# A linear-attention and gated-GLU training step on one core: features on partitions, folded attention values, one fused last layer, weight gradients at the end

## The chip, the core and the metric

The kernel runs on one core of a Trainium2 chip. The metric is the device time in microseconds (us). Runs of one kernel are compared through runs of the kernel before on the same chip in the same rounds. The ratios use fast runs alone.

## The reference, cut to what matters

Four layers are applied in turn to `x` of 2048 tokens by 512 features: linear attention (A), GLU (B), A, B. Both A layers share their weights, and so do both B layers. The kernel returns the output and the gradients of the input and of all five weights.

```python
def _A_ref(x, wqkv, wo):                   # 32 heads of 16
    q, k, v = ...                          # x @ wqkv
    phi = lambda t: where(t > 0, t + 1, exp(t)) + 1e-6
    kv = einsum("bhsd,bhse->bhde", phi(k), v)     # a sum over ALL tokens
    z = phi(k).sum over tokens                    # the same
    num, den = phi(q) @ kv, phi(q) @ z + 1e-6
    return (num / den) @ wo
def _B_ref(x, w_gate, w_up, w_down):       # 512 -> 1376 -> 512
    return (sigmoid(x @ w_gate) * (x @ w_up)) @ w_down
x = x + _A_ref(_layernorm(x), ...)         # layer 0
x = x + _B_ref(_layernorm(x), ...)         # layer 1
x = x + _A_ref(_layernorm(x), ...)         # layer 2
x = x + _B_ref(_layernorm(x), ...)         # layer 3
_out, _vjp = jax.vjp(f, ...); _grads = _vjp(grad_out)
```

What matters for the order of work: the attention sums run over all tokens. Nothing of layer 0's values can be finished before its keys are done for the last token, and the backward of an attention has two such sums as well. A program therefore falls into sweeps over the tokens with a seam between each two.

## The kernel before

It keeps tokens on partitions and takes 128 tokens at a time. Each matmul that contracts over features needs a turned operand, so activations and gradients are turned by TensorE with an identity, and ScalarE or VectorE copies them out of PSUM.

```python
def b_fwd(k, l, ln, ...):                       # one GLU layer, forward
    ...
        tps = ps_tp2.tile([P, 4, P], BF16, name="hhT_ps")
        for i, fc in enumerate(fcs):            # TensorE turns hh, 128 columns each
            nc.tensor.transpose(tps[0:r, i, :], hh_t[:, fc * P:fc * P + r], k.ident[:])
        nc.scalar.copy(hhT[:, fcs[0]:fcs[0] + nfull, :], tps[:, 0:nfull, :])
    ...
            nc.scalar.activation(ssd_t[:, 0, c0:c0 + w], g_ps[:, 0:w], ACT.Sigmoid)
            nc.scalar.activation(oms[:, 0:w], g_ps[:, 0:w], ACT.Sigmoid, scale=-1.0)
            nc.vector.tensor_tensor(hh_t[:, c0:c0 + w], u_ps[:, 0:w], ssd_t[:, 0, c0:c0 + w], ALU.mult)
            nc.gpsimd.tensor_tensor(ssd_t[:, 1, c0:c0 + w], hh_t[:, c0:c0 + w], oms[:, 0:w], ALU.mult)
    # [cut] ssd and hh are stored, and loaded again in the backward of the same layer

def p2_cols_group(k, R, lhs_all, set_t, W, dwp2d, out2d, c0, final):   # weight gradients of ONE layer
    if final:                                   # the second layer reloads the first one's partial sums
        R.eng().dma_start(out=av, in_=dwp2d[:, c0:c0 + W].rearrange("(c p) f -> p c f", p=P))
    # [cut] 16 matmuls per PSUM group, one per 128 tokens
        if not final:
            nc.scalar.copy(av[:, half * 2:half * 2 + 2, :], psv)
        else:
            nc.vector.tensor_tensor(ov[...], psv, av[...], ALU.add)
```

Of the kernel before, what the change touches and what calls it, by code (L numbers as in the profile page):

```python
# [11 lines left out]
ALU = mybir.AluOpType  # L12
AX = mybir.AxisListType
# [7 lines left out]
DH = 16  # L21
P = 128
NST = S // P
NDC = D // P
NFC = (F + P - 1) // P
FLAST = F - (NFC - 1) * P
FSL = [(0, 512), (512, 512), (1024, F - 1024)]
EPS_LN = 1e-5
EPS = 1e-6
NB = 4  # L30


def fchunks_of_slice(fs):
    c0, w = FSL[fs]
    return list(range(c0 // P, (c0 + w + P - 1) // P))


def fc_rows(fc):
    return FLAST if fc == NFC - 1 else P


def rows(st):
    return slice(st * P, (st + 1) * P)


class K:
    pass


@with_exitstack  # L50
def kernel(
# [18 lines left out]
    phases = "all"  # L70
    nc = tc.nc
    assert tuple(A_x.shape) == (1, S, D) and tuple(grad_out.shape) == (1, S, D)
    assert tuple(A_wqkv.shape) == (D, 3 * D) and tuple(A_wo.shape) == (D, D)
    assert tuple(B_w_gate.shape) == (D, F) and tuple(B_w_up.shape) == (D, F) and tuple(B_w_down.shape) == (F, D)
    k = K()
    k.nc, k.tc = nc, tc
    k.phases = phases

    x_in = A_x.rearrange("b s d -> (b s) d")
    g_in = grad_out.rearrange("b s d -> (b s) d")  # L80
    out0 = out_0.rearrange("b s d -> (b s) d")
    out1 = out_1.rearrange("b s d -> (b s) d")
# [3 lines left out]
    resid = ctx.enter_context(tc.tile_pool(name="resid", bufs=1))  # L86
    keep = ctx.enter_context(tc.tile_pool(name="keep", bufs=1))
    dram = ctx.enter_context(tc.tile_pool(name="dram", bufs=1, space=DRAM))
    k.keep = keep

    build_consts(k, consts)

    k.xs = [resid.tile([P, D], F32, name=f"x{st}") for st in range(NST)]

    def load_stream(io, src2d, b):
        stg_t = io.tile([P, NB, D], BF16, name="io_in")
        if b == 0:
            nc.sync.dma_start(out=stg_t[:, 0, :], in_=src2d[0:P, :])
            nc.sync.dma_start(out=stg_t[:, 1:NB, :],
                              in_=src2d[P:NB * P, :].rearrange("(n p) d -> p n d", p=P))  # L100
        else:
            nc.sync.dma_start(out=stg_t[:], in_=dram_batch(src2d, b))
        for j in range(NB):
            st = b * NB + j
            if j % 2 == 0:
                nc.vector.tensor_copy(k.xs[st][:], stg_t[:, j, :])
            else:
                nc.scalar.copy(k.xs[st][:], stg_t[:, j, :])
        return stg_t
    k.load_stream = load_stream  # L110

    def store_stream(io, dst2d, b):
        stg_t = io.tile([P, NB, D], BF16, name="io_out")
        for j in range(NB):
            st = b * NB + j
            nc.gpsimd.tensor_scalar(stg_t[:, j, :], k.xs[st][:], 1.0, 0.0, ALU.mult, ALU.add)
        nc.sync.dma_start(out=dram_batch(dst2d, b), in_=stg_t[:])
    k.store_stream = store_stream


    k.sv = {}
    for l in range(4):
        d = {}
        d["h"] = dram.tile([S, D], BF16, name=f"sv_h{l}")
        d["gbf"] = dram.tile([S, D], BF16, name=f"sv_gbf{l}")
        if l % 2 == 0:
            for nm in ("pq", "pk", "v", "o"):
                d[nm] = dram.tile([S, D], BF16, name=f"sv_{nm}{l}")
            d["dqkv"] = dram.tile([S, 3 * D], BF16, name=f"sv_dqkv{l}")
        else:  # L130
            d["ssd"] = dram.tile([S, 2, F], BF16, name=f"sv_ssd{l}")
            d["hdd"] = dram.tile([S, 3, F], BF16, name=f"sv_hdd{l}")
        k.sv[l] = d
    k.wT = dict(
        wqkvT=dram.tile([3 * D, D], BF16, name="wqkvT_d"),
        woT=dram.tile([D, D], BF16, name="woT_d"),
        wgT=dram.tile([F, D], BF16, name="wgT_d"),
        wuT=dram.tile([F, D], BF16, name="wuT_d"),
        wdT=dram.tile([D, F], BF16, name="wdT_d"),
    )  # L140
    k.dwp = dict(
        wqkv=dram.tile([D, 3 * D], BF16, name="dwp_wqkv"),
        wo=dram.tile([D, D], BF16, name="dwp_wo"),
        wg=dram.tile([D, F], BF16, name="dwp_wg"),
        wu=dram.tile([D, F], BF16, name="dwp_wu"),
        wd=dram.tile([F, D], BF16, name="dwp_wd"),
    )
    k.rstd = [keep.tile([P, NST], F32, name=f"rstd_all{l}") for l in range(4)]
    k.kv = {}

    k.A_wo = A_wo
    with tc.tile_pool(name="wfwd", bufs=1) as wfwd:
        k.wqkv = wfwd.tile([P, NDC, 3 * D], BF16, name="wqkv")
        with tc.tile_pool(name="io0", bufs=2) as io:
            load_stream(io, x_in, 0)
            nc.sync.dma_start(out=k.wqkv[:], in_=A_wqkv.rearrange("(c p) j -> p c j", p=P))
            for b in range(1, NST // NB):
                load_stream(io, x_in, b)
        k.wo = wfwd.tile([P, NDC, D], BF16, name="wo")
        nc.sync.dma_start(out=k.wo[:], in_=A_wo.rearrange("(c p) j -> p c j", p=P))  # L160
        k.wg = wfwd.tile([P, NDC, F], BF16, name="wg")
        nc.sync.dma_start(out=k.wg[:], in_=B_w_gate.rearrange("(c p) j -> p c j", p=P))
        k.wu = wfwd.tile([P, NDC, F], BF16, name="wu")
        nc.sync.dma_start(out=k.wu[:], in_=B_w_up.rearrange("(c p) j -> p c j", p=P))
        k.wd = wfwd.tile([P, NFC, D], BF16, name="wd")
        nc.sync.dma_start(out=k.wd[:, 0:NFC - 1, :],
                          in_=B_w_down[0:(NFC - 1) * P, :].rearrange("(c p) j -> p c j", p=P))
        nc.sync.dma_start(out=k.wd[0:FLAST, NFC - 1, :], in_=B_w_down[(NFC - 1) * P:F, :])

        with ExitStack() as lctx:  # L170
            k.lnres = dict(
                stg=lctx.enter_context(tc.tile_pool(name="ln_stg", bufs=2)),
                hT=lctx.enter_context(tc.tile_pool(name="ln_hT", bufs=4)),
                small=lctx.enter_context(tc.tile_pool(name="ln_small", bufs=6)),
                ps=lctx.enter_context(tc.tile_pool(name="ln_ps", bufs=1, space=PSUM)),
            )
            lns = [FwdLN(k, l) for l in range(4)]
            if phases != "fwd":
                wtg = wT_groups(k)
                half = 26  # L180
                with tc.tile_pool(name="wt_stage", bufs=2) as wt_stage:
                    a_fwd(k, 0, lns[0], nxt=lns[1],
                          extra=lambda ps_pool: [g(wt_stage, ps_pool) for g in wtg[:half]])
                b_fwd(k, 1, lns[1], nxt=lns[2])
                with tc.tile_pool(name="wt_stage2", bufs=2) as wt_stage:
                    a_fwd(k, 2, lns[2], nxt=lns[3],
                          extra=lambda ps_pool: [g(wt_stage, ps_pool) for g in wtg[half:]])
            else:
                a_fwd(k, 0, lns[0], nxt=lns[1])
                b_fwd(k, 1, lns[1], nxt=lns[2])  # L190
                a_fwd(k, 2, lns[2], nxt=lns[3])
            ostg = lctx.enter_context(tc.tile_pool(name="out0_stg", bufs=2))
            ocur = {}

            def out_cb(st):
                if st % NB == 0:
                    ocur["t"] = ostg.tile([P, NB, D], BF16, name="out0_t")
                nc.scalar.copy(ocur["t"][:, st % NB, :], k.xs[st][:])
                if st % NB == NB - 1:
                    nc.sync.dma_start(out=dram_batch(out0, st // NB), in_=ocur["t"][:])  # L200
            b_fwd(k, 3, lns[3], out_cb=out_cb)

    if phases == "fwd":
        return
    k.g_in = g_in
    k.g_from_input = 3
    k.sv[3]["gbf"] = g_in

    with ExitStack() as bctx:
        wb = bctx.enter_context(tc.tile_pool(name="wbwd", bufs=1))  # L210
        k.wb = wb

        def load_b_weights():
            k.wdT = wb.tile([P, NDC, F], BF16, name="wdT", tag="w_c")
            nc.sync.dma_start(out=k.wdT[:], in_=k.wT["wdT"].rearrange("(c p) f -> p c f", p=P))
            k.wuT = wb.tile([P, NFC, D], BF16, name="wuT", tag="w_a")
            k.wgT = wb.tile([P, NFC, D], BF16, name="wgT", tag="w_b")
            for t_sb, t_d in ((k.wuT, k.wT["wuT"]), (k.wgT, k.wT["wgT"])):
                nc.sync.dma_start(out=t_sb[:, 0:NFC - 1, :],
                                  in_=t_d[0:(NFC - 1) * P, :].rearrange("(c p) j -> p c j", p=P))  # L220
# [125 lines left out]
def wT_groups(k):  # L346
# [55 lines left out]
    return groups  # L402


NPRE = 2


class FwdLN:
# [701 lines left out]
```

## Time and profile before

| | before |
|---|---|
| time | 1395.17 us, 3 runs, 1393.22 to 1395.18 |
| TensorE matmuls | 9956, 3488 of them of 128 columns, 2840 of these turns with the identity |
| mean granted TensorE clock | 0.988 |

These are lines of the page of the kernel before. The first gives the span, the second each engine's busy time, share and number of instructions (PEld is the weight load, which overlaps PE). The two rows cut the span into 40 slices: busy tenths of TensorE, and the granted clock in tenths. The last row is what the DMA engines moved.

```profile
span 1393.1 us, 25045 instructions
PE 1297.9 (93%) x9956; PEld 790.1 (57%) x9956; DVE 679.9 (49%) x1468; ACT 647.3 (46%) x1168; POOL 250.5 (18%) x413
PE   4989899998899898998999999999999999988988
PEclk9999999999999999999999999999999999999999
DMA packets 268853, 269.77 MB, mean 194 GB/s; under 512 B 24576, under 2 KB 245184, under 8 KB 268736
```

TensorE is the limit. Its busy time overstates the work, since matmuls are pipelined and overlap. So I count *slots*: the distance from one start to the next in undisturbed rows of the timeline, 216 ns for 512 columns, 109 ns for 256 and 57 ns for 128. The 9956 matmuls are then worth about 1233 us. (The Trainium skill, "TensorE: Matmul & The Clock Gate", Part 1, gives N / 2.4 GHz + 2.5 ns, which is 215.7 ns for 512; the trace agrees.) What a stage takes beyond its slots I call its *excess*.

The one large wait of the kernel before lies in its last weight-gradient stage. In the chain of waits (start, length, what) it follows reloads of partial sums, and TensorE's timeline shows the gaps (in brackets: how long it stood idle, and what ended that). The chain runs through these reloads for some 34 us.

```profile
1223.27 9.33 DMA dw_stg<-dwp_wd
...
1235.63 11.10 DMA dw_stg<-dwp_wg
...
1249.65 9.64 DMA dw_stg<-dwp_wd
```

```profile
1233.47 11.94 PE L833 MATMUL p_ps<-p_set,p_a_15354 128*128 128x256 bf16 x96 [4.53 <-DVE dw_stg L798]
...
1260.16 2.08 PE L833 MATMUL p_ps<-p_set,p_a_15354 128*128 128x256 bf16 x9 [5.49 <-DVE dw_stg L798]
```

### The profile page before, as it was taken

Reading aid. Unit: us, or ns where it says so; the run is one execution under the profiler, and the core shown is the slowest. Engines: PE = TensorE matmul, PEld = TensorE weight load, DVE = VectorE, ACT = ScalarE, POOL = GpSimd, SP = SyncE. Lnnn points to the kernel's source line nnn. Section 1 sums busy time; section 2 is a strip of 40 time slices with the busy share of each in tenths; the row PEclk is TensorE's granted clock in tenths of the full one; section 3 lists DMA queues with packets and bytes.
Section 4 is the critical chain, followed back from the end, with each engine's and each line's share of the span. In section 5 each row is a group of like instructions: output and inputs, shape, how many; then the busy total and the mean of one; then the engine's idle time right before and its main releaser. Section 6 shows DMA issues by size and latency. Waiting matters only on the chain. (4 is left out here: it accounts for less than half of the span.)

```text
span 1393.1 us, 25045 instructions
## 1 busy us (share of the span) xinstructions
PE 1297.9 (93%) x9956; PEld 790.1 (57%) x9956; DVE 679.9 (49%) x1468; ACT 647.3 (46%) x1168; POOL 250.5 (18%) x413
## 2 busy tenths in 40 slices
PE   4989899998899898998999999999999999988988
PEld 2555455556455444554665677555548675556767
DVE  6664644567533355665857400456640676611111
ACT  5857576775776544443547411444431447600000
POOL 4026654105633300002100100010010101100000
PEclk9999999999999999999999999999999999999999
DMA  7622334452543497547774586964568956499745
GB/s 273 230 103 103 149 152 158 147 177 98 201 178 143 169 326 259 175 168 237 218 230 148 181 227 149 334 217 167 172 199 248 275 169 192 143 311 261 175 122 162
DMA packets 268853, 269.77 MB, mean 194 GB/s; under 512 B 24576, under 2 KB 245184, under 8 KB 268736
## 3 DMA queue, kind: packets, MB, share of 16 engines
q1 hardware_dynamic: 246272, 253.50, 57.2%
q10 hardware_dynamic: 22464, 14.68, 3.6%
q8 instruction: 78, 1.28, 0.4%
q14 instruction: 39, 0.32, 0.1%
HBM read 144.57 MB, written 123.57 MB: 192 GB/s over the span
## 5 line engine op out<-in xcount | busy, mean ns | idle before, releaser
L730 ACT COPY ddT<-T_ps 128x1024 bf16<-128x1024 bf16 (+1 forms) x96 | 83.1, 867 | 103.4 <-PE T_ps L728 103.3
L630 POOL TENSOR_TENSOR ssd_t<-hh_t,oms 128x512 bf16<-128x512 bf16 (+1 forms) x96 | 100.6, 1052 | 83.0 <-ACT oms L628 48.4
L648 DVE SCALAR_TENSOR_TENSOR junk<-t_sb,h_ld 128x512 bf16<-128x512 f32 x64 | 46.1, 720 | 137.6 <-ACT t_sb L646 136.6
L762 DVE TENSOR_TENSOR dd_t<-dhh_ps,ssd_ld 128x512 bf16<-128x512 f32 (+1 forms) x96 | 60.4, 629 | 102.0 <-PE dhh_ps L760 102.0
L742 PEld LDWEIGHTS <-ddT 128*128 128x128 bf16 (+1 forms) x704 | 66.3, 98 | 71.4 <-issue 12.5
L468 PE MATMUL mm_ps<-wqkv,hT 128*128 128x512 bf16 x384 | 100.2, 386 | 0.5 <-DVE x_108 L601 0.4
L742 PE MATMUL dh_ps<-wuT,ddT 128*128 128x512 bf16 (+1 forms) x352 | 96.5, 382 | 3.9 <-ACT t_sb L646 0.9
L833 PE MATMUL p_ps<-p_set,p_a_15354 128*128 128x256 bf16 (+1 forms) x768 | 82.5, 267 | 10.8 <-DVE dw_stg L798 10.8
L629 DVE TENSOR_TENSOR hh_t<-u_ps,ssd_t 128x512 bf16<-128x512 f32 (+1 forms) x96 | 60.7, 634 | 65.3 <-PE u_ps L624 50.3
L760 PE MATMUL dhh_ps<-wdT,gT 128*128 128x512 bf16 (+1 forms) x384 | 87.8, 364 | 5.0 <-DMA wdT<-wdT_d 4.3
L624 PE MATMUL u_ps<-wu,hT 128*128 128x512 bf16 (+1 forms) x384 | 92.4, 361 | 0.0
L621 PE MATMUL g_ps<-wg,hT 128*128 128x512 bf16 (+1 forms) x384 | 92.0, 361 | 0.4 <-DVE ostage L530 0.4
L833 PE MATMUL p_ps<-p_set,p_a_10151 128*128 128x256 bf16 (+1 forms) x768 | 81.5, 261 | 0.9 <-DMA p_set<-sv_hdd_130 0.9
L599 PE MATMUL y_ps<-wd,hhT 128*128 128x512 bf16 (+1 forms) x352 | 81.4, 380 | 0.0
L742 PE MATMUL dh_ps<-wgT,ddT 128*128 128x512 bf16 (+1 forms) x352 | 81.3, 379 | 0.0
L833 PEld LDWEIGHTS <-p_a_15354 128*128 128x128 bf16 x768 | 68.9, 100 | 21.7 <-issue 8.4
L590 ACT COPY hhT<-hhT_ps 128x512 bf16<-128x512 bf16 (+1 forms) x96 | 49.5, 515 | 58.3 <-PE hhT_ps L587 58.1
L728 PEld LDWEIGHTS <-dd_t 128*128 128x128 bf16 (+1 forms) x704 | 50.7, 101 | 40.8 <-DVE dd_t L762 18.5
L833 PEld LDWEIGHTS <-p_a_10151 128*128 128x128 bf16 x768 | 67.2, 98 | 9.2
L728 PE MATMUL T_ps<-ident,dd_t 128*128 128x128 bf16 (+1 forms) x704 | 66.4, 221 | 3.6 <-DVE dd_t L762 3.5
L838 DVE TENSOR_TENSOR dw_stg<-p_ps,dw_stg 128x512 bf16<-128x512 f32 (+1 forms) x36 | 23.4, 653 | 87.5 <-PE p_ps L833 74.4
L1038 PE MATMUL dh_ps<-wqkvT,dkvT 128*128 128x512 bf16 x256 | 65.6, 380 | 0.0
(493 smaller groups left out, 2498.3 us busy)
## 6 DMA issues: line engine op xcount, KB each, us to landing
p_set<-sv_hdd_130 SPq DMA_DIRECT2D x15, 1024.0 KB, 7.1
p_set<-sv_hdd_119 SPq DMA_DIRECT2D x15, 1024.0 KB, 6.3
sv_ssd_118<-ssd_t SPq DMA_DIRECT2D x16, 688.0 KB, 3.1
sv_ssd_129<-ssd_t SPq DMA_DIRECT2D x16, 688.0 KB, 3.1
ssd_ld<-sv_ssd_129 SPq DMA_DIRECT2D x16, 688.0 KB, 5.5
sv_hdd_130<-dd_t SPq DMA_DIRECT2D x16, 688.0 KB, 3.9
ssd_ld<-sv_ssd_118 SPq DMA_DIRECT2D x16, 688.0 KB, 6.0
sv_hdd_119<-dd_t SPq DMA_DIRECT2D x16, 688.0 KB, 3.7
```

The source lines that it names most:

```text
L468: nc.tensor.matmul(ps[:], lhsT=hT[:, kc, :], rhs=k.wqkv[:, kc, n * D:(n + 1) * D], start=(kc == 0), stop=(kc == NDC - 1))
L599: nc.tensor.matmul(y_ps[:], lhsT=T["hhT"][0:r, fc, :], rhs=k.wd[0:r, fc, :], start=(fc == 0), stop=(fc == NFC - 1))
L621: nc.tensor.matmul(g_ps[:, 0:w], lhsT=hT[:, kc, :], rhs=k.wg[:, kc, c0:c0 + w], start=(kc == 0), stop=(kc == NDC - 1))
L624: nc.tensor.matmul(u_ps[:, 0:w], lhsT=hT[:, kc, :], rhs=k.wu[:, kc, c0:c0 + w], start=(kc == 0), stop=(kc == NDC - 1))
L629: nc.vector.tensor_tensor(hh_t[:, c0:c0 + w], u_ps[:, 0:w], ssd_t[:, 0, c0:c0 + w], ALU.mult)
L630: nc.gpsimd.tensor_tensor(ssd_t[:, 1, c0:c0 + w], hh_t[:, c0:c0 + w], oms[:, 0:w], ALU.mult)
L728: nc.tensor.transpose(tps[0:r, a, i, :], dd[:, a, fc * P:fc * P + r], k.ident[:])
L730: nc.scalar.copy(ddT[:, :, fcs[0]:fcs[0] + nfull, :], tps[:, :, 0:nfull, :])
L742: nc.tensor.matmul(dh_ps[:], lhsT=T["ddT"][0:r, a, fc, :], rhs=wT[0:r, fc, :], start=(i == 0), stop=(i == n_mm - 1))
L760: nc.tensor.matmul(dhh_ps[:, 0:w], lhsT=gT[:, jc, :], rhs=k.wdT[:, jc, c0:c0 + w], start=(jc == 0), stop=(jc == NDC - 1))
L833: nc.tensor.matmul(psv[:, icl, :], lhsT=lhs_all[:, st, ic * P:(ic + 1) * P], rhs=set_t[:, st, 0:W], start=(st == 0), stop=(st == NST - 1))
L1038: nc.tensor.matmul(dh_ps[:], lhsT=lhsT, rhs=k.wqkvT[:, n * NDC + c, :], start=(i == 0), stop=(i == 3 * NDC - 1))
```

## The change

The kernel is rewritten with one aim: fewer TensorE slots. Features lie on partitions in blocks of 256 tokens, so most products need no turned operand. The value projection, the head-wise kv and the output projection are folded into one 512 x 512 matrix `Wp` per attention, made at the seam. The last GLU layer runs forward and backward in one sweep, so nothing of it is saved. The weight gradients of both layers accumulate in one PSUM group at the very end. The turns that remain necessary are mostly done by DMA. Each sweep is a software pipeline: every piece of a block gets a position in a written order, and the pieces are emitted sorted by it.

The diff is a rewrite of the file; this is its core, with cuts marked.

```diff
-def b_bwd_p2(k, R, l, final, ...):   # partial weight gradients per layer, reloaded for the second
+    def cols(hs_, srcs, out, c0, n, o0, scale):
+        sets = [tset(s_, c0, n) for s_ in srcs]            # DMA turns them: dma_start_transpose
+            for s_, h_ in zip(sets, hs_):                  # both layers, 32 matmuls, one PSUM group
+                    nc.tensor.matmul(ps[:, 0:n], lhsT=h_[st // 4][:, st % 4, cslice(m)], rhs=s_[:, st, 0:n], ...)
 # [cut]
+def a_barrier(k, l):                                       # a seam: after the sums over all tokens
+    # kv_ps <- wv, GTb;  kvT;  Wp[c] = kvT[c] @ wo[c];  Z from z
+def a_p2(k, l, b, xin_fn, x_out, at):                      # attention of one block
+    # den (TensorE) -> 1/den (VectorE) -> turn (TensorE) -> spread (TensorE) -> pn (VectorE) -> y (TensorE) -> x (VectorE)
+def layernorm(k, l, b, x_t):
+    # stats (VectorE) -> rstd (GpSimd) -> nmr (VectorE) -> h (ScalarE)
+def transpose_block(k, src, name, evac):
+    ps = tpps(k, [P, NDC, TB], name + "_ps")               # ONE PSUM bank for all such turns
 # [cut] glu_fwd, sweep 2
+        nc.vector.scalar_tensor_tensor(hh, th[:, 0:n], 1.0, flat(up[:])[:, 0:n], ALU.add, ALU.mult)
+        nc.gpsimd.tensor_scalar(s2, th[:, 0:n], 1.0, 1.0, ALU.mult, ALU.add)
+        nc.vector.scalar_tensor_tensor(t, th[:, 0:n], -1.0, hh, ALU.add, ALU.mult)
 # [cut] sweep2: written positions; t starts block b, ST2 = 22.5
+        u = t - (ST2 if b > 0 else 16)
+        a_p2(k, 0, b, ..., (u, u + 3, u + 5, u + 5.5, u + 8, u + 9))
+        L.add(u + 10, lambda b=b: ln1(b))                  # layernorm before the GLU of block b
+        L.add(u + 15, lambda b=b: tr1(b))                  # its turn on TensorE
+        glu_fwd(k, 1, b, lambda b=b: hTs.pop(b), x, t, ST2 / 6, 2)
+        v = t + ST2 * 7 / 6 + 0.5
+        L.add(v, lambda b=b: ln2(b))                       # layernorm of the next attention
+            a_k(k, 2, b, lambda b=b: h2.pop(b), (v + 5, v + 8, v + 10, v + 13, 2.0))
```

`th` is the tanh from which the sigmoid is made, `hh` the gated product that the GLU's last matmul (`y_acc`) reads, and `t`, one half of the tile `s2t`, is `(th - 1) * hh`, which only the backward needs. `hT`, `hTk`, `hTq` and `gT` are turned operands, of the layernorm output `h` and of a gradient.

The five sweeps are: (1) keys of layer 0; (2) attention 0, GLU 1, keys of layer 2; (3) attention 2, GLU 3 forward and backward, start of attention 2's backward; (4) its rest, GLU 1 backward, start of attention 0's backward; (5) its rest. Then come the weight gradients.

## The prediction

> **What bounds the kernel now.** TensorE. The page gives it 1298 us busy of 1393 (93%), VectorE 49%, ScalarE 46%. Busy overstates it, so I use start-to-start slots from the timeline and the chain of waits: 64 matmuls of 512 columns take 13.83 us (216 ns each), 128 of 256 columns 13.97 us (109 ns), four 128-column transposes about 0.23 us (57 ns each). With these slots the 9956 matmuls need about 1233 us. The other 160 us: 18 us before the first matmul (timeline), about 34 us at 1223-1259 in the last weight-gradient stage waiting for reloaded partial gradients (chain of waits), and some 105 us of short waits in the stages, with a granted clock of 0.988.
>
> **What the change does to TensorE.** The instruction order shows 7820 matmuls. At the same slots: 1081 us, 152 less. Removed: nearly all transposes (3488 matmuls of 128 columns become 692), the forward value projection, the last GLU layer's separate forward and backward sweeps (one sweep computes both, so nothing is saved and reloaded), the weight transposes. Weight gradients keep their columns, but accumulate both layers in one group of 32 matmuls, so the partial gradients, their reloads and the 34 us wait disappear. By stage: sweep 1 46 us, sweep 2 190, sweep 3 293, sweep 4 212, sweep 5 49, weight gradients 292.
>
> **What it adds.** About 70 MB of crossbar transposes by DMA, of 235 MB in all (before: 268 MB, none transposed), on one queue. VectorE gets denser per block of 256 tokens. With slots from the old trace (512 columns from PSUM 0.60 us, 256 with accumulator read about 0.44, an f32 SBUF operation about 0.7) I estimate 4.7 us per block in sweep 1 (TensorE 4.4), 20 in sweep 2 (22), 31 in sweep 3 (36), 20 in sweep 4 (26), 6 in sweep 5 (7). TensorE should stay the limit except in sweep 1, but sweeps 1, 2 and 5 have little slack. ScalarE and GpSimd fall below half. Sigmoid as tanh leaves one activation table load instead of four.
>
> **The DMA risk.** The weight-gradient stage eats one transposed set of 2.0-2.9 MB per 14-19 us, about 150 GB/s, plus 12 MB of untransposed operands: around 200 GB/s over 292 us. The old trace moved 239 GB/s in such a stage (480-610 us) with plain reads. Its trace has no transposes; "DMA: Bandwidth & Descriptors" of the Trainium skill (latency table) gives 261 GB/s for DMA transposes with a non-contiguous middle dimension. That suffices, without much margin; I allow 15 us.
>
> **Sum (estimate).** 1081 / 0.988 = 1094; start 18; last evacuation and store 5; five global barriers (short dependent chains, partly filled) 20; waits in the sweeps, 3-4% of 790 us, 28; starving transposes 15. Total 1180 us.
>
> Predicted: **1180 us**, 8 in 10 between 1125 and 1265. Faster by over 2%: 0.93; within 2%: 0.04; slower: 0.03.
>
> **What would show each step.** Right: TensorE near 93% of about 1180 us, some 7820 matmuls, weight loads far fewer; a final stage of about 300 us with TensorE over 90% busy; VectorE about 65% of the span and at most 90% in sweep 2; first matmul at about 18 us. Wrong: matmuls of the weight gradients waiting for the transposed sets; long VectorE releases of the PSUM tiles in sweep 2; a clock well below 0.98.
>
> **What would make it wrong.** Transposes slower than 150 GB/s (at 100 GB/s the last stage lengthens by some 130 us, and the total approaches 1310); plain transfers queueing behind transposes, so that sweeps wait for loads; scalar_tensor_tensor on bf16 running at full PSUM cost and making sweep 2 VectorE-bound (adds 10-20 us); barriers longer than 4 us each because their chains alternate between engines.

## The result, and the profile after

| | before | after |
|---|---|---|
| time, median (range) | 1394.29 us (1393.22 to 1395.18, 4 runs) | 1290.8 us (1287.81 to 1293.33, 4 runs) |
| ratio to before | 1 | 0.926, 95% interval 0.924 to 0.928 |
| mean granted clock | 0.988 | 0.959 |

A ratio is the mean time of one kernel's fast runs over that of the other's fast runs of the same rounds, so it is not quite the ratio of the medians. The change is faster by 7.4%, but 111 us slower than predicted and outside the predicted range.

The same lines of the page, after:

```profile
span 1291.6 us, 20232 instructions
PE 1148.8 (89%) x7820; PEld 732.7 (57%) x7820; DVE 704.5 (55%) x1654; ACT 358.7 (28%) x610; POOL 88.1 (7%) x215
PE   4769888896799889989996999999688999999998
PEclk9989999897899999899997999999799999999999
DMA packets 469104, 235.89 MB, mean 183 GB/s; under 512 B 285232, under 2 KB 453392, under 8 KB 466960
```

The work is as predicted: 7820 matmuls, worth 1081 us of slots. The excess is not: 1291.6 - 1081.1 = 210.5 us, where the prediction had 99. The PEclk row shows something new too, slices at 0.7 and 0.8. Summed over the span, 52.4 us of clock were lost, against some 17 before.

I cut the trace into stages at the first matmul of a kind (first product of a seam, first gate product of sweep 2's GLU, first product with the turned gradient in sweeps 3 and 4, and so on) and took span less slots:

| stage (after) | span | slots | excess | lost clock in it |
|---|---|---|---|---|
| start and sweep 1 | 63.1 | 33.0 | 30.1 | 0.0 |
| seam 1 | 28.1 | 13.0 | 15.1 | 3.4 |
| sweep 2 | 238.0 | 182.4 | **55.6** | 17.1 |
| seam 2 | 17.9 | 7.5 | 10.5 | 3.3 |
| sweep 3 | 332.1 | 289.8 | **42.3** | 10.3 |
| seam 3 | 25.0 | 10.9 | 14.1 | 4.4 |
| sweep 4 | 216.8 | 200.9 | 15.9 | 7.6 |
| seam 4 and sweep 5 | 68.3 | 52.0 | 16.2 | 3.4 |
| weight gradients | 297.5 | 291.4 | 6.0 | 1.7 |
| tail | 5.0 | 0.2 | 4.8 | 1.2 |

The clock's record begins at 19.5 us. Before that the first eight products of 512 columns start 427 ns apart, which is half rate, so the 0.0 of the first row is too low. Of the 52.4 us, some 42 fell on matmuls (an estimate: the slots of the 435 matmuls that started at half clock). The rest fell on time in which TensorE stood still, and the column is part of the excess, not an addition to it.

The weight gradients, which I had feared for, lose almost nothing: the reloads and their wait are gone, and the turned sets arrive in time. The excess lies in sweeps 2 and 3 and at the seams. Here is TensorE's timeline around a block seam of sweep 3 (start, length, instruction, count):

```profile
522.11 0.38 PE L766 MATMUL dh_acc<-wgT,dg 128*128 128x512 bf16 x1
525.54 1.01 PE L237 MATMUL hT_ps<-ident,h 128*128 128x128 bf16 x8 [3.05 <-ACT gT L240]
526.34 1.92 PE L425 MATMUL q_ps<-hTq,wq 128*128 128x256 bf16 x8
528.05 1.91 PE L716 MATMUL g_ps<-hT,wg 128*128 128x256 bf16 x8
...
533.22 1.04 PE L425 MATMUL q_ps<-hTq,wq 128*128 128x256 bf16 x8
```

TensorE stands still for 3.05 us before the turn of the layernorm output `h`. The eight products after it then take 1.71 us from start to start (526.34 to 528.05), and eight such products 0.88 us from 533.22 on (the next row starts at 534.10): half the rate. So the stall costs nearly twice its length. This is no single case. After the clock's record begins, TensorE stood still for 2.6 us or more twelve times. Each time 3.4 to 10.2 us at half clock began, during the stall or within 0.8 us of its end. ScalarE's timeline at that time shows why the wait is put down to the copy of `gT`: that copy sits in its queue behind the layernorm of this block, which came late, and both turns share one PSUM bank.

```profile
523.07 1.52 ACT L263 ACTIVATE h<-xa,ln_nmr,rstd 128x512 bf16<-128x512 f32 x2 [4.24 <-DVE ln_nmr L261]
524.50 0.99 ACT L240 COPY gT<-gT_ps 128x1024 bf16<-128x1024 bf16 x1
```

These are TensorE's longest waits in the first seven of sweep 2's eight blocks (who waited for whom, us in total, times, longest):

```profile
PE hT_ps L237 <- ACT h L263: 9.0, 10, 1.6
PE y_acc L747 <- DVE hh L740: 4.7, 5, 1.3
PE ya_ps L490 <- DVE pnT L477: 4.1, 5, 0.9
```

And this is a seam, from the last block of sweep 2 to the first gate product of sweep 3:

```profile
302.52 0.40 PE L237 MATMUL hTk_ps<-ident,h 128*128 128x128 bf16 x4 [4.71 <-ACT h L263]
...
304.94 3.60 PE L301 MATMUL k_ps<-wk,hTk 128*128 128x512 bf16 x8 [1.10 <-ACT hTk L240]
...
315.69 2.89 PE L425 MATMUL q_ps<-hTq,wq 128*128 128x256 bf16 x16 [2.73 <-DMA hTq<-h_d]
320.20 0.24 PE L446 MATMUL den_ps<-Z,pqT 128*128 128x32 bf16 x2 [1.62 <-DVE pqT L274]
...
341.17 1.31 PE L237 MATMUL hT_ps<-ident,h 128*128 128x128 bf16 x8 [3.29 <-ACT h L263]
343.64 1.86 PE L716 MATMUL g_ps<-hT,wg 128*128 128x256 bf16 x8 [1.16 <-ACT hT L240]
```

Every line ends in a wait for another engine. It is one chain that goes round them, and in the written order nothing else stands there to be done.

### The profile page after: what moved, and what is told of

Its sections match the earlier page's. It is cut to its first block, busy times and chain, and to the rows that moved or that the text cites. A ratio compares the mean times of both kernels' runs of the same rounds, so it can differ in the third digit from the quotient of the medians.

```text
span 1291.6 us, 20232 instructions
## 1 busy us (share of the span) xinstructions
PE 1148.8 (89%) x7820; PEld 732.7 (57%) x7820; DVE 704.5 (55%) x1654; ACT 358.7 (28%) x610; POOL 88.1 (7%) x215
## 4 chain that ended last, share of the span: by engine, by line
PE 52%; DVE 9%; DMA 5%; issue 3%; SPq 2%; ACT 2%; POOL 1%; DVEq 0%; ACTq 0%
PE dw_ps L1194 10%; PE dw_acc L1194 5%; PE dhh_ps L716 4%; PE dh_acc L766 4%; PE dh_acc L764 4%; PE dw_ps L1182 4%; PE dha_ps L681 4%; PE g_ps L716 3%; PE u_ps L716 2%; PE dpn_ps L528 2%; DMA pkT<-pk_d 2%; PE y_ps L829 2%; PE dw_acc L1182 2%; PE m_ps L562 2%; PE dpk_ps L665 1%
## 5 line engine op out<-in xcount | busy, mean ns | idle before, releaser
L764 PE MATMUL dh_acc<-wuT,du 128*128 128x512 bf16 x352 | 132.3, 379 | 5.4 <-DVE du L797 4.7
L766 PE MATMUL dh_acc<-wgT,dg 128*128 128x512 bf16 x352 | 132.5, 379 | 0.9 <-DVE dg L798 0.9
L716 PE MATMUL g_ps<-hT,wg 128*128 128x256 bf16 x704 | 97.1, 280 | 2.3 <-ACT hT L240 2.3
L716 PE MATMUL u_ps<-hT,wu 128*128 128x256 bf16 x704 | 97.0, 279 | 0.0
L716 PE MATMUL dhh_ps<-gT,wdT 128*128 128x256 bf16 x704 | 93.3, 274 | 1.1 <-ACT gT L240 1.1
L716 PEld LDWEIGHTS <-wg 128*128 128x128 bf16 x704 | 70.4, 101 | 28.0 <-issue 3.1
L716 PEld LDWEIGHTS <-wdT 128*128 128x128 bf16 x704 | 69.5, 99 | 19.5 <-issue 1.3
L716 PEld LDWEIGHTS <-wu 128*128 128x128 bf16 x704 | 70.4, 100 | 11.1
L1194 PEld LDWEIGHTS <-h3a 128*128 128x128 bf16 x512 | 50.1, 98 | 25.4 <-issue 0.9
L1194 PEld LDWEIGHTS <-h1a 128*128 128x128 bf16 x512 | 50.1, 98 | 24.7
L1182 PEld LDWEIGHTS <-dw_set 128*128 128x128 bf16 (+1 forms) x352 | 35.2, 100 | 40.8
```

The lines of the kernel that those rows point to most:

```text
L716: nc.tensor.matmul(ps[:, i, :], lhsT=w[:, m, fsl(fc)], rhs=rhsT[:, m, :], start=(m == 0), stop=(m == NDC - 1))
L764: nc.tensor.matmul(st["acc"][j][:], lhsT=du[:, i, tslice(j)], rhs=k.wuT[:, fc, :], start=(fc == 0), stop=False)
L766: nc.tensor.matmul(st["acc"][j][:], lhsT=dg[:, i, tslice(j)], rhs=k.wgT[:, fc, :], start=False, stop=(fc == NFC - 1))
L1182: nc.tensor.matmul(ps[0:r, :], lhsT=s_[:, st, c0:c0 + r], rhs=g_[st // 4][:, st % 4, :], start=(i == 0), stop=(i == 31))
L1194: nc.tensor.matmul(ps[:, 0:n], lhsT=h_[st // 4][:, st % 4, cslice(m)], rhs=s_[:, st, 0:n], start=(i == 0), stop=(i == 31))
```

## The experiments

Theories: **order** (each engine works in order, and at the seam of two blocks TensorE reaches a product before the chain through the other engines has made its operand); **VectorE capacity** (sweeps 2 and 3 give VectorE more than it can do); **seams** (serial chains between the sweeps cost far more than the 20 us allowed); **clock** (each stall is followed by some microseconds at half rate). That VectorE, ScalarE and GpSimd execute strictly in order is stated by the Trainium skill, "Perfetto Trace Analysis", Per-engine timelines; the timeline of e8 agrees for GpSimd.

Times are medians of 4 runs; "ratio" is to the kernel before, with 0.926 for the changed kernel. The pages of e9 to e12, e16 and e17 lack about 1% of the matmul records (7713 of 7820 in e9), so for those I compare only spans of stages, not slots. Microseconds of VectorE work taken away or added are sums of the operations' durations (48 operations of up to 0.69 us in each sweep, 96 in both; the expectation of e4 says 88). Runs with a wrong result are marked. Their outputs are wrong, which doesn't matter for the times.

### e1: start the next block's chain earlier

```diff
-        u = t - (ST2 if b > 0 else 16)
+        u = t - (ST2 + 5 if b > 0 else 16)
-        u = t - (ST3 if b > 0 else 24)
+        u = t - (ST3 + 10 if b > 0 else 24)
```

> Edit: in sweeps 2 and 3 the chain of the next block (attention denominators, values, layernorm, its turn on TensorE) is put earlier in the written order, by 5 of 22.5 us in sweep 2 and 10 of 36 us in sweep 3; no work added or taken away. In-order latency theory (TensorE reaches the turn of the layernorm output before VectorE and ScalarE have made it, at the seam of two blocks): sweeps 2 and 3 lose 30 to 60 of their 87 us above the sum of matmul slots, the time falls to 1230 to 1260 us. VectorE capacity theory (VectorE has too much work in these sweeps): no gain, 1285 to 1295 us. Barrier theory: no gain here.

Measured: 1279.7 us (1275.85 to 1279.91), ratio 0.917. Sweep 3 became 17.3 us shorter (332.1 to 314.8), sweep 2 did not move (238.0 to 237.8). So order is at work in sweep 3, without a single operation less. The time lies outside the ranges of both theories. The gain is below what I expected, since the stall partly turned into a new one. In sweep 3 the waits for the turn of `h` fell from 13.7 us (12.7 for the bank held by `gT`, 1.0 for `h`) to 4.0, and a wait for the queries' turned load appeared (same columns as above):

```profile
PE q_ps L425 <- DMA hTq<-h_d: 7.8, 4, 3.0
PE hT_ps L237 <- ACT h L263: 4.0, 7, 1.0
```

All these transfers are issued by SyncE, in order. Its timeline (SPq: what its sequencer issues, and how long that took) shows the load coming last, behind stores of fresh results and another turned load, where TensorE ran out of work at 433 us:

```profile
428.93 2.53 SPq L517 DMA_TRANSPOSE pn<-pnT_d  x1
431.57 0.53 SPq L700 DMA_DIRECT2D du_d<-du  x1
432.19 0.41 SPq L700 DMA_DIRECT2D dg_d<-dg  x1
432.66 1.23 SPq L404 DMA_TRANSPOSE hTq<-h_d  x1
```

### e2: the gradient's turn gets another PSUM bank

```diff
-    ps = tpps(k, [P, NDC, TB], name + "_ps")
+    ps = (mmps if name == "gT2" else tpps)(k, [P, NDC, TB], name + "_ps", BF16)
```

> Edit: the turn of the gradient in sweep 3 (gT2) writes one of the five matmul banks in place of the single transpose bank, so the turn of the layernorm output no longer has to wait until ScalarE has copied the gradient's turn out. If the single transpose bank is what stops TensorE for 3 us in each block of sweep 3 (and the half clock after it costs as much again): sweep 3 loses 25 to 40 us, time 1250 to 1268. If the wait is only a sign of ScalarE or VectorE being late, TensorE stops at the next thing: time within 8 us of 1291.

Measured: 1287.2 us (1285.12 to 1291.99), ratio 0.923; sweep 3 3.3 us shorter. This is the second expectation, and its runs overlap those of the changed kernel. The bank that the profile names is not the cause. With it free, TensorE waited 10.3 us for `h` itself in that sweep, where it had waited 12.7 us for the copy of `gT`: a wait was renamed.

### e3: the seams no longer depend on the sums (wrong)

```diff
-            nc.scalar.copy(GTb[:, m, :], A.GT[:, m, :])
+            nc.scalar.copy(GTb[:, m, :], k.wk[:, m, :])
 # [cut] likewise z, MT and the two accumulators of the backward
```

> Wrong results on purpose: the four seams between sweeps take their matrices from weights that lie ready and constants, in place of the sums over all blocks, so the next sweep need not wait for the last block of this one; all the same matmuls, copies and stores are done. Barrier theory (serial chains at the seams cost 60 us, not the 20 that I allowed): the time falls by 40 to 60 us, to 1230 to 1250. If the seams cost what I allowed: falls by under 20 us.

Measured: 1283.3 us (1279.59 to 1285.99), ratio 0.919. That is under the 20 us of the second expectation. Seams 1 and 2 kept their spans (27.9 and 18.0 us). The 7 us are spread, 2 in each of sweeps 2 and 3 and 3 at seam 3. The work kept its place in the written order, so the run says little about the seams.

### e4: an operation of VectorE is left out (wrong)

```diff
-        nc.vector.scalar_tensor_tensor(t, th[:, 0:n], -1.0, hh, ALU.add, ALU.mult)
 # [cut] the same in sweep 3; hh or s2 is used in its place
```

> Wrong results on purpose: the VectorE operation that makes (tanh-1)*hh is left out in sweeps 2 and 3 (88 operations of 0.69 us and less, about 30 us of VectorE in each sweep; hh or tanh+1 is used in its place; same matmuls and bytes). VectorE capacity theory: sweeps 2 and 3 get 40 to 60 us shorter, time 1230 to 1250. In-order latency theory (chain at the seam of two blocks, VectorE idle during some of the stalls): under 20 us, time above 1270.

Measured: 1266.9 us (1264.62 to 1269.07), ratio 0.908, between the two expectations. Sweep 2 lost 16.8 us, sweep 3 11.1 us, of 30 us of VectorE taken away in each. VectorE counts, but less than one for one.

### e5: e3, with the seams' work also written earlier (wrong)

```diff
-    L.add(tb, lambda: a_barrier(k, 2))
+    L.add(tb - 45, lambda: a_barrier(k, 2))
 # [cut] the other seams by 16 to 50 us
```

> As e3 (wrong on purpose: the seams' matrices come from weights and constants), but the work of the four seams is now also written 16 to 50 us earlier, inside the sweep before; in e3 it kept its place, so e3 said little. Seam theory (serial chains at the seams: the end of the last block, the barrier's products, the first block of the next sweep; I count about 93 us above the slots there): the time falls by 35 to 60 us, to 1230 to 1255, with most of it at the seams after sweeps 1, 2 and 3. If the products of the barriers themselves are cheap and only the drain of the last block costs: falls by 10 to 20 us.

Measured: 1299.4 us (1291.93 to 1303.27), ratio 0.931: slower than the changed kernel. The seam's products did move into the sweep before, but the wait was the same. From the start of sweep 2 to that of sweep 3 it took 259.8 us, against 255.9. TensorE now waited for the lead of the first block: loads of the turned `h`, queries, denominators, values, layernorm, turn. Neither expectation came. The theory fell as I had put it: to take away the dependence on the sums, and to move the products of the barrier, gained nothing.

### e6: the VectorE operation twice

```diff
+        nc.vector.scalar_tensor_tensor(t, th[:, 0:n], -1.0, hh, ALU.add, ALU.mult)   # again, in sweeps 2 and 3
```

> The opposite of e4: the VectorE operation that e4 left out is done twice in sweeps 2 and 3 (about 30 us more of VectorE in each, same results). e4 gave back 17 us in sweep 2 and 11 us in sweep 3. VectorE on the path of these sweeps: sweep 2 gets 18 to 30 us longer, sweep 3 11 to 25 us, time 1320 to 1345. If VectorE only mattered by where a single operation stood: under 15 us in all.

Measured: 1310.6 us (1304.78 to 1315.7), ratio 0.939. Sweep 2 grew by 11.5 us and sweep 3 by 7.1 us for 30 us more in each, less than I had given for VectorE being on the path all the time, and together more than the 15 us of the other expectation. So about a quarter to two fifths of each added microsecond shows. That fits an engine that is in the way at certain moments.

### e7: the same operation written later

```diff
-        nc.vector.scalar_tensor_tensor(t, th[:, 0:n], -1.0, hh, ALU.add, ALU.mult)
 # [cut] in y(p), two chunks later:
+        nc.vector.scalar_tensor_tensor(flat(st["s2t"][:, 1, cs, :]), flat(st["s2t"][:, 0, cs, :]), -2.0, ...)
```

> Sweep 2 alone: the operation that e4 left out is kept, but written two chunks later (from tanh+1 in bf16 less 2), behind the operation that TensorE waits for; same amount of VectorE work. Queue theory (VectorE has time enough on average, but works in order, and what TensorE needs stands behind what only a store needs): sweep 2 loses 8 to 17 of its 35 us above the slots in blocks 1 to 7, time 1274 to 1283. Capacity theory (VectorE is short of time): no gain, 1287 to 1293.

Measured: 1290.9 us (1288.09 to 1293.61), ratio 0.925: no gain, a miss for the queue theory in this form. By itself it lies in the range of the capacity theory; e13b below decides between the two. Sweep 2 took 238.2 us. TensorE's waits stayed as they were: 8.5 us for the layernorm's turn (9.0 before) and 4.2 for `hh` (4.7). Two chunks later, the operation stands before another one that is needed; this is my reading and was not tested.

### e8: the same operation on GpSimd

```diff
-        nc.vector.scalar_tensor_tensor(t, th[:, 0:n], -1.0, hh, ALU.add, ALU.mult)
+        nc.gpsimd.tensor_scalar(t, th[:, 0:n], 1.0, -1.0, ALU.mult, ALU.add)
+        nc.gpsimd.tensor_tensor(t, t, hh, ALU.mult)
```

> Sweep 2 alone: the same operation is moved from VectorE to the almost idle GpSimd, as two operations there; 30 us less of VectorE, same results. Either VectorE theory: sweep 2 gets 10 to 17 us shorter, as in e4, time 1274 to 1281. If GpSimd is too slow, or the layernorm's small operations on GpSimd now stand behind these: sweep 2 the same or longer, 1290 to 1310.

Measured: 1290.0 us (1285.88 to 1291.92), ratio 0.924; sweep 2 only 2.4 us shorter, with 30 us less on VectorE. GpSimd's timeline shows where the gain went:

```profile
181.21 0.22 POOL L256 TENSOR_SCALAR rstd<-ln_mv 128x2 f32<-128x2 f32 x1
181.51 0.62 POOL L742 TENSOR_SCALAR s2t<-th 128x512 bf16<-128x512 f32 x1
182.09 0.71 POOL L257 TENSOR_TENSOR rstd<-rstd,neghalf 128x2 f32<-128x2 f32 x1
```

The layernorm's two small operations stand on both sides of a new one. TensorE's wait for `hh` fell from 4.7 to 1.1 us, its wait for the layernorm's turn rose from 9.0 to 11.2 us. This was the first hint that the sum of an engine's work is the wrong measure, and the position of a few operations the right one.

### e9: order put right in three places

```diff
+        (e1's earlier chain)
-        if hf == 0:
-            ld()
+    k.L.add(at[0] - 8, ld)                 # the queries' load, 8 us before its product
+    ps = (mmps if name in ("gT2", "hTk") else tpps)(...)
```

> All corrections of order, none of work: e1's earlier chain, the queries' turned loads issued 8 us earlier than their products (e1 turned the stall for the layernorm's turn into a wait of 2 to 3 us for these loads, which stand in the queue behind the store of h), and the turns of hTk and gT2 in the matmul banks (e1 waits 6.2 us for the single bank). In-order latency theory: sweep 2 loses 10 to 20 us, sweep 3 16 to 22 us against the changed kernel, time 1253 to 1268. VectorE capacity theory: no better than e1, 1275 to 1280.

Measured: 1256.9 us (1255.84 to 1258.01), ratio 0.902, in the range of the order theory. But the gain lies in sweep 3 (27.3 us); sweep 2 with its seam gave 3.5. In the first seven blocks of sweep 2 TensorE now waited six times for `hh`, up to 3.1 us each. The first line is from the list of its waits (us in total, times, longest), the second is one such stall:

```profile
PE y_acc L746 <- DVE hh L739: 14.5, 6, 3.1
120.73 0.39 PE L746 MATMUL y_acc<-wd,hh 128*128 128x512 bf16 x1 [2.82 <-DVE hh L739]
```

VectorE's timeline just before it:

```profile
116.64 1.28 DVE L254 BATCH_NORM_STATS2 ln_stats<-xa 128x6 f32<-128x512 f32 x2
117.84 0.16 DVE L255 BATCH_NORM_AGGREGATE ln_mv<-ln_stats 128x2 f32<-128x6 f32 x1
117.92 0.66 DVE L254 BATCH_NORM_STATS2 ln_stats<-xa 128x6 f32<-128x512 f32 x1
...
118.58 0.66 DVE L254 BATCH_NORM_STATS2 ln_stats<-xa 128x6 f32<-128x512 f32 x1
119.79 0.16 DVE L261 SCALAR_TENSOR_TENSOR ln_nmr<-ln_mv,rstd 128x2 f32<-128x2 f32 x1 [0.56 <-POOL rstd L257]
...
120.02 0.65 DVE L739 SCALAR_TENSOR_TENSOR hh<-th,u_ps 128x512 bf16<-128x512 f32 x1
```

The statistics of two layernorms, of the next block and of the block just finished, stand together in front of the `hh` that TensorE needs. In the written order they coincide: e1 had moved the first to where the second was. That is a burst. VectorE even stands idle for 0.56 us in it: the layernorm's next operation waits for GpSimd, and `hh`, whose inputs are there since TensorE's products at 116, waits behind it.

### e10: e9 with e8's move to GpSimd

```diff
+        (e9, and the two GpSimd operations of e8)
```

> e9 with e8's move of the operation to GpSimd. In e8 the wait of TensorE for hh fell, but the wait for the layernorm's turn rose, since its small operations on GpSimd stood behind the new ones; with the chain started earlier that has slack. If both theories hold together (VectorE late for hh, and the chain at the seam): 8 to 15 us below e9, 1240 to 1256. If capacity does not count: within 4 us of e9.

Measured: 1264.5 us (1260.59 to 1265.05), ratio 0.906: 7.6 us slower than e9, a miss. Sweep 2 took 234.9 us against 228.2, although VectorE had less to do. TensorE waited for `hh` as before (14.2 us, 14.5 in e9), and VectorE's wait for the layernorm's `rstd` from GpSimd rose from 7.5 to 12.0 us. Other operations could then stand behind that one; how much of the 7.6 us this is was not tested.

### e11: e5 with the first block's lead written earlier (wrong)

```diff
+        (e5, and)
-        u = t - (ST3 if b > 0 else 24)
+        u = t - (ST3 if b > 0 else 40)
 # [cut] sweep 2's first block by 4 us, the queries at both seams by 6 and 11 us
```

> As e5 (wrong on purpose), with the first block's lead of sweeps 2 and 3 (queries, denominators, values, layernorm) written earlier too, by 4 to 6 us at the first seam and 11 to 16 us at the second. In e5 the products of the barrier had moved away, and TensorE then waited for that lead's own chain: 29 us from the first denominator to the first gate product, nothing else to do. Seam theory as mended (what costs is the chain of the first block after all sums, not the products): the second seam loses 12 to 30 us against e5, time 1265 to 1288. If not: as e5, 1295 to 1303.

Measured: 1299.9 us (1298.25 to 1302.45), ratio 0.933: as e5, a miss. The written order said earlier, but the queries' loads still landed after the last block's `h` (TensorE waited 3.64 us for the first), so the chain started no sooner.

### e12: useless matmuls in the stalls

```diff
+def warm(k, w, n):
+    ps = mmps(k, [P, D], "warm_ps")
+    for i in range(n):
+        k.nc.tensor.matmul(ps[:], lhsT=w[:, i % NDC, 0:P], rhs=w[:, i % NDC, :], start=(i == 0), stop=(i == n - 1))
+            L.add(v + 1.9, lambda: warm(k, k.wo, 18))     # and 18 each before two other first turns
```

> The changed kernel with 54 useless matmuls of 512 columns (11.7 us at full rate) in three stalls at the seams: before the first turn of sweep 2, before the turn of sweep 2's last block, and before the first turn of sweep 3. Nothing reads them. Clock theory (each stall of TensorE of 3 us or more is followed by some 3.5 us at half clock, so it costs more than it lasts): the matmuls after these stalls run at full rate, and the time falls by 4 to 9 us, to 1282 to 1287, in spite of the added work. If the half clock does not come from the stalls: 0 to 12 us longer, 1291 to 1303.

Measured: 1288.2 us (1281.97 to 1292.91), ratio 0.924, between the two expectations and in range of the changed kernel's runs: 11.7 us of added work cost nothing that shows, and a gain is not resolved. In the profiled run, the fastest of the four, the lost clock fell from 52.4 to 35.2 us; 5.2 of this are in sweep 3, which had no useless work in it. The same place as in the seam above, with the stall filled:

```profile
296.76 4.05 PE L405 MATMUL warm_ps<-wo 128*128 128x512 bf16 x17
301.64 0.40 PE L237 MATMUL hTk_ps<-ident,h 128*128 128x128 bf16 x4 [0.83 <-ACT h L263]
...
303.85 1.90 PE L301 MATMUL k_ps<-wk,hTk 128*128 128x512 bf16 x8 [1.10 <-ACT hTk L240]
...
314.87 3.57 PE L431 MATMUL q_ps<-hTq,wq 128*128 128x256 bf16 x16 [5.09 <-DMA hTq<-h_d]
```

The eight key products take 1.90 us in place of 3.60. So the half rate comes from the stall before it. Part of this gain is given back at once, in a longer wait for the load (5.09 in place of 2.73 us). The Trainium skill, "TensorE: Matmul & The Clock Gate", Part 1, gives half rate after an idle window of about 3.4 us, and the full rate again after a busy one. The trace agrees on the length: its spells of half clock last 3.4, 6.8 or 10.2 us. But no window had to be idle throughout. In the twelve stalls of the changed kernel TensorE was busy for 0.1 to 1.3 us of the 3.4 us before the spell began. Nor is a stall of 3 us a sure sign: in e13b one of 3.1 us was followed by no half clock.

### e13 and e13b: the second layernorm of sweep 2 moved by 6 and by 10 us

```diff
+        (e9, and)
-        L.add(v, lambda b=b: ln2(b))
+        L.add(v + (10 if b < NBLK - 1 else 0), lambda b=b: ln2(b))
+            a_k(k, 2, b, lambda b=b: h2.pop(b), (v + 5 + 10, v + 8 + 10, v + 10 + 10, v + 13 + 10, 2.0))
```

> e9 with the second layernorm of sweep 2 (for the next attention) and what hangs on it written 6 us later, so that it does not meet the first layernorm of the next block: in e9 VectorE worked 11 us without a pause there, and TensorE waited about 3 us per block for hh behind it. Burst theory (VectorE has time on average, not at the seam): sweep 2 loses 8 to 20 us against e9, time 1238 to 1250. Capacity theory: no gain, 1254 to 1260.

> As e13_spread6 with 10 us in place of 6. Burst theory: again 1238 to 1250, and about the same as with 6. Capacity theory: 1254 to 1260.

Measured: 1243.2 us (1241.16 to 1244.31), ratio 0.890, with 6; 1236.4 us (1234.16 to 1237.16), ratio 0.886, with 10. Both results are correct. The second lies below its expected range, which named no difference between 6 and 10 us. Sweep 2 fell from 228.2 us in e9 to 216.6 and to 210.0. VectorE's timeline of e13b at the same seam:

```profile
116.96 1.28 DVE L254 BATCH_NORM_STATS2 ln_stats<-xa 128x6 f32<-128x512 f32 x2
118.16 0.17 DVE L255 BATCH_NORM_AGGREGATE ln_mv<-ln_stats 128x2 f32<-128x6 f32 x1
118.24 0.66 DVE L739 SCALAR_TENSOR_TENSOR hh<-th,u_ps 128x512 bf16<-128x512 f32 x1
...
118.91 0.66 DVE L254 BATCH_NORM_STATS2 ln_stats<-xa 128x6 f32<-128x512 f32 x1
```

`hh` now stands in the middle at 118.24, and TensorE does not stop for it: in the list of its waits in sweep 2's blocks 1 to 7 the wait for `hh` is gone, and the largest is this one.

```profile
PE hT_ps L237 <- ACT h L263: 4.8, 7, 1.2
```

No VectorE operation was removed: its page has 1654, as the changed kernel's. Its share *rose*, from 69% (164.6 of 238.0 us) to 76% (158.9 of 209.9 us) in sweep 2, while the excess there fell from 55.6 to 28.2 us. That settles it against capacity. The edit moves the layernorm together with the keys that hang on it (turn, products and what VectorE does with them), and which of these matters most was not separated.

### e14: e9 with e4's operation left out (wrong)

```diff
+        (e9, and e4's edit)
```

> Wrong on purpose: e9 with e4's VectorE operation left out in sweeps 2 and 3. Capacity theory: the rest of the loss in both sweeps goes too: 25 to 35 us below e9, 1222 to 1232. Burst or order theory: sweep 3, now in order, gains under 6 us; sweep 2 gains 8 to 15; 1236 to 1248.

Measured: 1242.5 us (1240.8 to 1243.72), ratio 0.890. Sweep 3 gained 5.5 us and sweep 2 10.1 us against e9, as the burst theory had it. Taking 60 us off VectorE is worth less (14.3 us) than moving one layernorm and its keys by 10 us (20.5 us, e13b).

### e15: the first GLU block of three sweeps fed from elsewhere (wrong)

```diff
+            L.add(t - 26, lambda: (gT3(0), hTs.__setitem__(-1, load_hT(k, 2, 0, "hTx"))))
+        glu_both(k, 3, b, lambda b=b: hTs.pop(b) if b else hTs.pop(-1), ..., t - (0 if b else 20), ST3 / 6, 2)
 # [cut] likewise in sweeps 2 and 4
```

> Wrong on purpose: the changed kernel, with the GLU of the first block of sweeps 2, 3 and 4 fed from tensors stored long before (a turned load each, 3 of 256 KB more) and written 8, 20 and 12 us earlier, so that TensorE has work while the attention chain of that first block runs; all the chain's own work is still done, and the sums are still waited for. Lead theory (the seams cost since nothing but one chain through five engines can run there): the three seams lose 20 to 40 us, time 1250 to 1271. If it is the barrier products or the loads that hold the seams: under 8 us, above 1283.

Measured: 1284.2 us (1281.17 to 1287.04), ratio 0.920: 6.6 us, a miss for the lead theory. In number it is the second expectation, but that expectation's reason did not hold. The first product with the turned gradient in sweep 3 did start 17.7 us earlier (329.3 in place of 347.0), but the sweep's end came only 5.8 us earlier. The first block took 40.4 us in place of 27.8, and TensorE then waited for the chain of the *second* block:

```profile
363.89 1.31 PE L237 MATMUL hT_ps<-ident,h 128*128 128x128 bf16 x8 [4.08 <-ACT h L263]
366.31 1.87 PE L716 MATMUL g_ps<-hT,wg 128*128 128x256 bf16 x8 [1.10 <-ACT hT L240]
```

The wait was put off by one block. I read this as the filling of a pipeline, which a start for one block does not do.

### e16 and e17: e13b with the queries in the drain of sweep 2, and with useless matmuls besides

```diff
-        a_q(k, 2, b, (tb - 14 + 2 * b, tb - 13 + 2 * b))
+        a_q(k, 2, b, (tb - 30 + 2 * b, tb - 29 + 2 * b))
+            L.add(u + 14.9, lambda: warm(k, k.wo, 18))    # e17 only, and before the first turn of sweep 3
```

> e13b_spread10 with the queries of the next attention's first four blocks (64 products, 7 us) written 16 us earlier, so that they fill the stall for the turn of sweep 2's last block (2.8 and 1.1 us in e13b, then k and q at half clock). Results stay right. Drain theory: 5 to 10 us less at this seam, 1226 to 1232. If the rest of the chain only starts no sooner: under 3 us, 1233 to 1239.

> e16 with 36 useless matmuls (7.8 us at full rate) before the first turn of sweep 2 and before that of sweep 3. Clock theory: 2 to 5 us below e16 in spite of the work. If not: 0 to 8 us above it.

Measured: e16 1238.5 us (1234.87 to 1244.25), ratio 0.888, no gain over e13b and a miss. e17 1234.9 us (1232.57 to 1235.5), ratio 0.885: 3.6 us below e16 with 7.8 us of added work. This agrees with the clock theory, though the ranges touch. e13b and e17 cannot be told apart in time. e13b is the version to keep: the fastest without useless work, and 4.2% faster than the changed kernel (1236.4 against 1290.8 us).

## Why the prediction was wrong

**Right.** TensorE's slots: 7820 matmuls, 1081 us, as counted. The weight-gradient stage: 297.5 us (about 300 predicted), and the reloads are gone, with a wait that was 34 us long in the chain but 12.2 us on TensorE. The DMA risk did not come: the stage moved 190 GB/s on average, its excess was 6.0 us of the 15 allowed, and waits for turned sets came to 0.7 us. The 261 GB/s that the prediction took from the Trainium skill, "DMA: Bandwidth & Descriptors", Latency and other measured facts, was not put to the test, for the stage never needed that rate. The tail cost 4.8 us (5 predicted). The start was shorter than predicted: 12.3 us to the first layernorm turn, not 18. The risk that `scalar_tensor_tensor` on bf16 runs at full cost came true (see the last section), and so did "barriers longer than 4 us each": the seams lost 10.5 to 15.1 us each.

**Wrong: the step that failed.** It is this part of the sum: "five global barriers (short dependent chains, partly filled) 20; waits in the sweeps, 3-4% of 790 us, 28", together with the clock of 0.988. The mechanism was named, and its size was wrong: the sweeps' waits were 131.6 us and not 28, the seams 55.9 and not 20, and the clock 0.959.

| term | predicted | measured (clock loss included) |
|---|---|---|
| clock, as a term of its own | 13 | 52.4, spread over the rows below |
| start and tail | 23 | 12.3 + 4.8 = 17.1 |
| waits in sweeps 1 to 4 | 28 | 17.8 + 55.6 + 42.3 + 15.9 = 131.6 |
| seams, with sweep 5 | 20 | 15.1 + 10.5 + 14.1 + 16.2 = 55.9 |
| weight gradients | 15 | 6.0 |
| together | 99 | 210.6 |

**Where 54 of the 111 us went: order, not capacity.** I had taken the 3 to 4% from an overall feel for short waits, although I had counted some 105 us of them in the old kernel, over 8% of its slots. I had checked VectorE only by its sum per block (20 us against 22 of TensorE in sweep 2). The sum was fine. What TensorE met was local: at each block seam the chain of denominators, values, layernorm and turn goes through VectorE, GpSimd, ScalarE and back, behind other work in in-order queues. e13b does the same operations in another order and takes sweeps 2 and 3 from 97.9 to 43.6 us of excess. These 54.3 us are nearly all of its gain, 54.4 us by the medians (1290.8 to 1236.4) and 59.5 between the two profiled runs. 17.4 of them are lost clock (27.4 to 10.0). e4, e6 and e14 show that VectorE's load counts, but with a fifth to somewhat over half of each microsecond; in e2, e7, e8 and e10 it did not help to free a bank, to delay an operation or to move one to GpSimd. e9 changed three things at once; of these only the earlier chain (e1) and a free bank (e2) were tried alone, and e13b's own move was tried only on top of e9.

**The clock.** I used one mean clock from the old kernel. It did not carry over, since it went with the stalls. In e13b the lost clock is 34.1 us, with no change but order; in e12 the products after a filled stall ran at full rate.

**What stays open: the other 57 us.** In e13b's profile the seams with sweep 5 still hold about 56 us (20 predicted), as in the changed kernel, and sweeps 1 to 4 about 72 (28 predicted). Some 30 of these 72 are in the last blocks of sweeps 2, 3 and 4, where no next block runs beside them (in the changed kernel it was 19.5 us for sweep 2 alone). In e3, e5 and e11 neither the dependence on the sums nor the place of the seams' own products set this. e15 shows that work for one block in the gap is mostly given back at the next block's chain. The traces read as one chain through four engines and the load queue, which must be filled before two blocks overlap. No run made a seam cheap, so this reading is not shown to be the whole cause.

Smaller points: weight loads are not "far fewer" per matmul. There is still one for each of the 7820, 732.7 us in place of 790.1. TensorE was at 89% and not 93% of the span, VectorE at 55% and not 65%, for the span was longer and VectorE's work smaller than estimated.

## What to carry to other kernels

When a change removes work from the busiest engine, cost what is left by the chains at block seams, not by the other engines' totals: list what each in-order queue holds in front of the operation that the busy engine waits for. A wait that the profile names may only be the last link; freeing that link (e2) renamed it, and moving the start of the chain (e1) cut it from 13.7 to 4.0 us in sweep 3. Before unloading an engine, move the operations that bunch together: here one layernorm with its keys, moved by 10 us, was worth more than leaving out 60 us of VectorE work. Count a TensorE stall of about 3 us twice: in the changed kernel all twelve of 2.6 us or more brought half clock, for 6.5 us on average, a loss of up to 3.3 us each.

## What the Trainium skill lacked or had wrong

- "TensorE: Matmul & The Clock Gate", Part 1, says that for modeling the ramp penalty is under 1% of a typical kernel's span. The sentence stands with the ramp at a kernel's start, and the same Part goes on to kernels whose stalls recur, so it is not wrong but must not be taken for a kernel like this one. Here stalls recur at block seams, and 52.4 us of 1291.6 (4.1%) of clock were lost, some 42 of them on matmuls (estimate). With e13b's order it was 34.1 of 1232.1 us (2.8%).
- "VectorE: DVE Perf Modes", The perf-mode tier table, lists `tensor_tensor` with 2x on bf16 but has no row for `scalar_tensor_tensor`. With bf16 output, one f32 and one bf16 input in SBUF, 128x512 took 684 to 689 ns, the same as with a PSUM operand (678 ns), while `tensor_tensor` on bf16 took 418 ns. With bf16 alone (e7: two inputs in SBUF and the output) it took 680 ns, no faster.
- "DMA: Bandwidth & Descriptors", Issuing engines are not separate DMA queues, says that the time to initiate a DMA is usually small relative to the DMA itself. In e1 the issue of the queries' turned load of 256 KB took 1.2 to 1.8 us, where it landed after 3.3 to 4.8 us. The page names no cost of the order of issues on one engine: in e1's sweep 3 TensorE lost 7.8 us in four waits for loads that were issued last.
